# Separate row buffers for every other batch of q and k, in memory that the first batch's rows leave, and later places for the loads and DMA transposes

## The chip, the cores and the metric

One Trainium2 chip, one core of it. The metric is the device time of one launch in microseconds (us). The kernel before takes 309.26 us, the median of three runs (307.13 to 311.13).

## What is computed

Attention with a sliding window, and then a two-layer projection of all tokens. From the reference:

```python
# q, k, v: (8 batches, 8 heads, 576 positions, 64)
scores = scale * np.matmul(q, k.transpose(0, 1, 3, 2))
mask = np.abs(pos[:, None] - pos[None, :]) <= 32
attn = softmax(np.where(mask, scores, -1e9))
attn_out = np.matmul(attn, v)
...
x = attn_out.transpose(0, 2, 1, 3).reshape(4608, 512)
h = x @ w_in                                   # 512 -> 2048
g = where(h >= 1, h, where(h <= -1, 0, (h + 1) ** 2 / 4))
out = g @ w_out                                # 2048 -> 512
```

## The kernel before, in words

**One main loop.** The loop variable `a` at line 497 counts 144 steps of projection work (18 blocks of 256 tokens, 8 steps a block) and 16 more for the rest of the output. A step multiplies a piece of the hidden layer (lines 491 or 516), brings it through ScalarE and VectorE (lines 535 to 542), and then issues the attention work that is entered for this step and a few matmuls of the second layer (line 451 in `unit`). The attention of batch b is thus spread over the projection of the batches before it. The order of every engine's instructions is written out by hand: `at(a, ...)` enters work for a step, and `run(a)` issues it.

**Where q and k come from.** Scores need q and k with head dimension on the partitions: the tiles `qT` (three of them, in turn) and `kT` (three). For batch 0 and 1 TensorE transposes the rows. For batch 2 to 7 the way has two parts:

- `load_nat(b, t)` (line 95) loads the rows of q (t = 0) or k (t = 1) in their natural order into a tile `qn` or `kn` of 4,608 bytes a partition, with two DMAs (line 99) from the POOL queue; each also casts float32 to bfloat16. `load_v` (line 102) loads v with four DMAs.
- `xpose(b, t)` (line 196) turns such a tile into `qT` or `kT` with one DMA transpose (line 198) from the SP queue.

The scores of a batch (line 231) are the readers of `kT`. The first of them for batch 2 to 7 stand in steps 26, 38, 52, 68, 86 and 104.

**Where the work is entered.** For batch 3 to 7 the loads of q, k and v are entered at the step of that batch's first scores less 17, 16 and 15; the two transposes 6 and 8 steps after the first of these, which is 11 and 9 steps ahead of the first scores. The transposes of batch 2 stand at steps 16 and 18, and its loads ahead of the loop. POOL does nothing in the loop but issue loads, so the step of a load does not hold it back: POOL issues loads one after the other, each as soon as its buffer is free. The SP queue issues two things, in program order: the transposes, and the DMAs of finished output (`out`, lines 456 and 472). Each output DMA waits for the ScalarE copy (`osb`, lines 455 and 471) that makes its data. Output DMAs of the part that matters are entered in steps 27, 31, 35, 39, 45, 50, 55, 61, 66, 71, 75, 79 and every fourth after that. Inside a step the output comes ahead of the transpose.

**Row buffers.** There are two buffers for q and k rows, tags `n0` and `n1`. The tag is `n{(b + t) % 2}`, so q of batch b takes the buffer in which k of batch b-1 was, and k of batch b that of q of batch b-1. A load of batch b therefore waits for the transposes of batch b-1. `vn` has three buffers, so v of batch b waits for the last attention work of batch b-3.

**Batch 0's memory.** A pool named `early` holds what only the start needs: the rows of batch 0 (`q32`, `qh`, `kh`, `qb`) and a small tile `step`, together about 16.6 KB a partition. It stays open to the end of the kernel. Its last readers are the TensorE transposes of step 1.

Of the kernel before, what the change touches and what calls it, by code (L numbers as in the profile page):

```python
# [8 lines left out]
BF = mybir.dt.bfloat16  # L9
# [5 lines left out]
def kernel(  # L15
# [20 lines left out]
    B, H, S, D = q.shape  # L36
# [3 lines left out]
    NU = NY * S // 128  # L40
# [8 lines left out]
    nat = ctx.enter_context(tc.tile_pool(name="nat", bufs=2))  # L49
# [26 lines left out]


    qn, kn, vn = {}, {}, {}
    HD = (slice(0, 64), slice(64, 128))

    def load_half(half, t, h, eng=None, x=None):
# [12 lines left out]

    def load_nat(b, t):
        src, dst, nm = ((q, qn, "qn"), (k, kn, "kn"))[t]
        x = dst[b] = nat.tile([128, NU, 2, D], BF, name=nm, tag=f"n{(b + t) % 2}", bufs=1)
        for h in range(2):
            nc.gpsimd.dma_start(out=x[:, :, h], in_=src[b, NY * h:NY * h + NY].rearrange("y s d -> (y s) d")  # L99
                                .rearrange("(u p) d -> p u d", p=128))  # L100

    def load_v(b, n):
        if b not in vn:
            vn[b] = nat.tile([128, 2 * NC, 2, D], BF, name="vn", tag="vn", bufs=3)
        h, a = divmod(n, 2)
        y = NY * h + 2 * a
        nc.gpsimd.dma_start(out=vn[b][64 * a:64 * a + 64, :, h], in_=v[b, y:y + 2].rearrange("y s d -> (y s) d")  # L107
                            .rearrange("(c r) d -> r c d", r=64))
# [8 lines left out]
        nc.gpsimd.dma_start(out=w_out[:, k0:k1, 256 * c:256 * c + 256],  # L117
                            in_=moe_w_out.rearrange("(ko ki) f -> ki ko f", ki=128)[:, k0:k1, 256 * c:256 * c + 256])

    early = ctx.enter_context(tc.tile_pool(name="early", bufs=1))  # L120
    q32 = early.tile([128, 2, S], FP, name="q32")
    for h in range(2):
        load_half(0, 0, h, (nc.sync, nc.scalar)[h], q32)
# [21 lines left out]
    def put(todo):  # L145
        for fn, *x in todo:
            fn(*x)
# [7 lines left out]
    put([(load_v, 1, n) for n in range(4)])  # L155
    P.tensor_copy(band[HD[1], 0:128], band[HD[1], 64:192])
    for m, n, x in ((mask4, 8, 128), (mask8, 4, TAIL)):
        P.tensor_copy(m.rearrange("p (n j) -> p n j", n=n),
                      band[:, :x].rearrange("p (n j) -> p n j", n=1).to_broadcast([128, n, x]))
    put([(load_w_out, 1, 8 * n, 8 * n + 8) for n in range(2)])  # L160
    put([(load_nat, 2, t) for t in range(2)] + [(load_v, 2, n) for n in range(4)])


# [9 lines left out]
    def tpose(b, n, t, copy, ps):  # L173
# [14 lines left out]
        for j in range(j0, j1):  # L188
            if isinstance(src, list):
                for h in range(2):  # L190
                    nc.tensor.transpose(ps[HD[h], j - j0], src[h][:, D * j:D * j + D], ident)  # L191
            else:
# [3 lines left out]
    def xpose(b, t):  # L196

        nc.sync.dma_start_transpose(out=qkT(b, t).rearrange("d (u p) -> d u p", p=128),
                                    in_=(qn, kn)[t][b].rearrange("p u h d -> p (u h d)"))
# [7 lines left out]
    def add_mask(ps, n, w):  # L207
        for a in range(2):
            for h in range(2):
                nc.tensor.matmul(ps[h][HD[a], :n * w].rearrange("p (n j) -> p n j", n=n), ident[HD[h], HD[h]],  # L210
                                 bias[HD[h], 64 * h:64 * h + w].rearrange("p (n j) -> p n j", n=1)
                                 .to_broadcast([64, n, w]),
                                 start=True, stop=False, skip_group_check=True)

    def scores(b, ys, pars, cs, eng, pool=ps_s, w=128, ready=None):
# [8 lines left out]
        for y1 in range(*ys):  # L224
            for par in range(*pars):
                for c2 in range(*cs):
                    c = 2 * c2 + par
                    for a in range(2):
                        for h in range(2):
                            s0 = S * (y1 + 2 * a) + 64 * c  # L230
                            nc.tensor.matmul(ps[HD[a], h, w * n:w * n + w], kT[b][HD[h], s0:s0 + 64],  # L231
                                             qTs[b % 3][HD[h], PAD + s0 - 32:PAD + s0 - 32 + w],
                                             start=eng is not None, stop=True, skip_group_check=True)
# [81 lines left out]
    def flush():  # L315
        while muls:
            muls.pop(0)()
# [9 lines left out]
    def tposes(b, *sets):  # L327

        todo = []
        for (t, half), pool, copy in zip(sets, (ps_s, ps_n), (A.copy, V.tensor_copy)):  # L330
            tp = pool.tile([128, 2, 8, 128], BF, name="tp", tag="bb")
            todo += [tpose(b, 2 * half + part, t, copy, tp[:, part]) for part in range(2)]
        for copy in todo:
            copy()
# [78 lines left out]
    sl = [30, 32, 35, 38, 41, 44, 47, 50, 52, 57, 60, 63, 66, 68, 72, 76, 79, 82, 86]  # L413
# [4 lines left out]
        at(10 + 1.5 * t, (tposes, 1, (t, 0), (t, 1)))  # L418
    loads, xps = {}, {16: [(2, 0)], 18: [(2, 1)]}
    for b in range(LONG + 1, B):  # L420
        a = sl[5 * (b - 1) - 7] - 17
        for t in range(3):
            loads.setdefault(a + t, []).append((b, t))
        for t in range(2):
            xps.setdefault(a + 6 + 2 * t, []).append((b, t))
# [3 lines left out]
    def home(t):  # L429

        return (3 - t % 4 if t % 4 in (0, 3) else t % 4) if WIDE[0] <= NF * t < WIDE[1] else t % 4
# [43 lines left out]
    def run(pos):  # L475
        todo = []
        for fn, *x in ev.get(pos, []):
            if fn is sums:
                todo.append(sums(*x))
            elif fn is tposes:  # L480
                tposes(*x)
            else:
                pool = (x.pop(),) if x[-1] in (ps_s, ps_n, ps_o) else ()
                fn(*x, eng, *pool)
        for end in todo:
            end()

    def project(hp, f, r0, todo, first, last):

        for n, (j, kk) in enumerate(todo):  # L490
            nc.tensor.matmul(hp[:, j], w_in[:, kk, 256 * f + 128 * j:256 * f + 128 * j + 128],  # L491
                             xT[:, kk, r0:r0 + TB], start=first and n == 0, stop=last and n == len(todo) - 1,
                             skip_group_check=True)
# [3 lines left out]
    for a in range(NF * NB + 2 * NF):  # L497
        wide = WIDE[0] <= a < WIDE[1]
        eng = None if a < 14 else V
        post = [] if a >= 40 else [x for n, x in pairs if n == a] + [a - NF] * (a >= 2 * NF + 2)  # L500
        for b, x in loads.get(a, []):
            if x < 2:
                load_nat(b, x)
            else:
                for n in range(4):
                    load_v(b, n)
        if a == 0 or a > 3:
            flush()
        if a < NF * NB:
            if wide:  # L510
                n, f = divmod(a - WIDE[0], 2 * NF)
                t = WIDE[0] // NF + 2 * n
                r0 = TB * t % RING
                hp = ps_h.tile([128, 2, TB], FP, name="hp", tag="hp")
                for n, kk in enumerate((0, 2, 1, 3)):
                    nc.tensor.matmul(hp.rearrange("p n t -> p (n t)"), w_in[:, kk, 128 * f:128 * f + 128],  # L516
                                     xT[:, kk, r0:r0 + 2 * TB], start=n == 0, stop=n == 3)
                g = gT[:, f, home(t):home(t + 1) + 1:home(t + 1) - home(t)]
            else:
                t, f = divmod(a, NF)  # L520
                r0 = TB * t % RING
                if a in (0,):
                    hps = [ps_h.tile([128, 2, TB], FP, name="hp", tag="hp") for _ in range(2)]
                    for y in range(2):
                        for n in range(2):
                            project(hps[n], f + n, r0, [(j, y + 2 * m) for j in range(2) for m in range(2)], y == 0, y == 1)
                elif not hps:
                    pool, tag = (ps_o, "op") if a == 6 else (ps_h, "hp")
                    hps = [pool.tile([128, 2, TB], FP, name="hp", tag=tag)]
                    project(hps[0], f, r0, [(j, kk) for j in range(2) for kk in (0, 2, 1, 3)], True, True)  # L530
                hp = hps.pop(0)
                g = gT[:, 2 * f:2 * f + 2, home(t)]

            rr = ewp.tile([128, 2, TB], FP, name="rr")
            A.activation(rr, hp, AF.Relu, scale=0.5, bias=0.5)  # L535
            mx = ewp.tile([128, 2, TB], FP, name="mx")
            if a in two_on_act:
                A.activation(mx, rr, AF.Square)
                V.scalar_tensor_tensor(g, hp, 1.0, mx, op0=ALU.max, op1=ALU.min)
            else:  # L540
                V.tensor_max(mx, hp, rr)  # L541
                V.scalar_tensor_tensor(g, rr, 1.0, mx, op0=ALU.min, op1=ALU.mult)  # L542
        flush()
        run(a)
        for x in post:
            if x < 16:
                pair(x)
            else:
                for j in range(4):
                    unit(4 * x + j)  # L550
        if a >= 40:
            n = 3 if a < 72 else 4
            for x in range(done, done + n):
                unit(x)
            done += n
        run(a + 0.5)
        for x in xps.get(a, []):
            xpose(*x)

# [29 lines left out]
```

## Time and profile before

| | |
|---|---|
| runs | 307.13, 309.26, 311.13 us |
| the profiled execution: its own time | 308.08 us |
| its span, first to last instruction | 306.3 us |
| granted TensorE clock | 1.0 throughout |
| ACT, POOL busy | 190.6 us, 78.2 us |
| bytes moved by DMA | 35.67 MB |

The span is what the trace shows; 1.8 us of the execution's time lie outside it. "Busy" is time in which an engine ran an instruction; for POOL and SP the issuing of DMAs lies on the queue's sequencer. A row of the chain of waits or of the list of waits such as `PE bb L231 <- DMA kT<-kn` says that TensorE stood still ahead of line 231 until a DMA that writes `kT` from `kn` had landed. In a list of waits the numbers are the total in us, how often, and the longest.

### The profile page before, as it was taken

How to read it: one execution, taken by the hardware profiler on the slowest of the kernel's cores; microseconds unless marked ns; L12 is line 12 of the kernel's file. 1: busy time of each engine (PE TensorE's matmuls, PEld its weight loads, DVE VectorE, ACT ScalarE, POOL GpSimd, SP SyncE). 2: the span in 40 equal slices, each digit the busy share in tenths (PEclk: the TensorE clock that was granted, in tenths of full speed). 3: DMA queues.
4: the chain of work that ended last, by engine and by line, in shares of the span. 5: the costliest groups of instructions: out<-in, count | busy, mean ns of one | idle time of the engine just before them, and what ended most of it. 6: DMA issues, size and time to landing. Idle time of an engine off the chain costs nothing.

```text
span 306.3 us, 7848 instructions
## 1 busy us (share of the span) xinstructions
PE 298.4 (97%) x3324; PEld 175.0 (57%) x3324; DVE 241.8 (79%) x378; ACT 190.6 (62%) x318; POOL 78.2 (26%) x94
## 2 busy tenths in 40 slices
PE   8889999999999999999999999999999999999995
PEld 3567878876666776544444444444445444446644
DVE  4278958879888999999988888888888888788700
ACT  3687796648757767667766766665667654444311
POOL 8896661037008204601800730000000000000000
PEclk9999999999999999999999999999999999999999
DMA  9999999989999996997999997551011000000121
GB/s 153 184 195 201 178 185 179 165 152 159 127 155 145 151 142 122 171 155 121 147 154 177 108 170 77 113 112 36 34 36 37 34 36 35 34 36 34 58 81 68
DMA packets 137331, 35.67 MB, mean 116 GB/s; under 512 B 122320, under 2 KB 133072, under 8 KB 137296
## 3 DMA queue, kind: packets, MB, share of 16 engines
q0 software_dynamic: 103136, 18.06, 80.2%
q1 hardware_dynamic: 34016, 16.81, 26.8%
q8 instruction: 26, 0.43, 0.6%
q10 hardware_dynamic: 144, 0.29, 0.4%
q14 instruction: 9, 0.07, 0.1%
HBM read 36.70 MB, written 9.44 MB: 151 GB/s over the span
## 4 chain that ended last, share of the span: by engine, by line
PE 85%; DMA 8%; POOL 3%; ACT 1%; issue 1%; DVE 0%; POOLq 0%; ACTq 0%
PE op L451 34%; PE hp L516 23%; PE hp L491 14%; DMA kT<-kn 7%; PE bb L297 5%; PE op L466 5%; PE bb L231 2%; DMA w_in<-in_moe_w_in_dram 2%; POOL w_in L112 1%; PE op L442 1%; POOL vn L107 1%; PE tp L191 1%; POOL kh L86 1%; POOL qh L86 0%; PE bb L210 0%
## 5 line engine op out<-in xcount | busy, mean ns | idle before, releaser
L535 ACT ACTIVATE rr<-hp 128x512 f32<-128x512 f32 x144 | 85.5, 595 | 84.5 <-PE hp L516 49.5
L451 PE MATMUL op<-w_out,gT 128*128 128x512 bf16 x496 | 126.9, 380 | 0.0
L541 DVE TENSOR_TENSOR mx<-hp,rr 128x512 f32<-128x512 f32 x139 | 95.8, 689 | 26.7 <-ACT rr L535 24.9
L542 DVE SCALAR_TENSOR_TENSOR gT<-rr,mx 128x512 bf16<-128x512 f32 x139 | 96.4, 694 | 4.8
L516 PE MATMUL hp<-xT,w_in 128*128 128x512 bf16 x320 | 82.1, 379 | 0.0
L451 PEld LDWEIGHTS <-gT 128*128 128x128 bf16 x496 | 46.1, 98 | 47.6
L491 PE MATMUL hp<-xT,w_in 128*128 128x256 bf16 x512 | 66.2, 273 | 1.7 <-DMA w_in<-in_moe_w_in_dram 1.5
L491 PEld LDWEIGHTS <-w_in 128*128 128x128 bf16 x512 | 49.2, 98 | 17.0 <-DMA w_in<-in_moe_w_in_dram 1.3
L516 PEld LDWEIGHTS <-w_in 128*128 128x128 bf16 x320 | 31.3, 98 | 37.8
L99 POOL DMA_DIRECT2D qn<-in_q_dram x12 | 14.6, 1222 | 92.2 <-DMA kT<-kn 90.1
L239 ACT ACTIVATE pt<-bb 128x1024 bf16<-128x1024 f32 (+1 forms) x33 | 32.9, 1002 | 6.1 <-PE bb L231 4.7
L107 POOL DMA_DIRECT2D vn<-in_v_dram x32 | 27.5, 893 | 5.1 <-DMA w_out<-in_moe_w_out_dram 2.9
L309 DVE TENSOR_TENSOR xT<-bb,rc 128x512 bf16<-128x512 f32 (+1 forms) x32 | 21.0, 657 | 9.8 <-ACT rc L304 8.9
L455 ACT COPY osb<-op 128x512 f32<-128x512 f32 x31 | 18.0, 581 | 12.4 <-PE op L451 12.1
L304 ACT ACTIVATE rc<-lr 128x512 f32<-128x512 f32 (+2 forms) x40 | 23.5, 587 | 1.3
L303 ACT ACTIVATE lr<-bb 128x512 f32<-128x512 f32 (+2 forms) x40 | 22.0, 550 | 0.2
L205 DVE TENSOR_TENSOR pt<-pt,mask 128x1024 bf16<-128x1024 bf16 (+1 forms) x33 | 20.3, 615 | 0.8 <-ACT pt L239 0.7
L297 PE MATMUL bb<-pt,ones 64*64 64x256 bf16 (+3 forms) x352 | 19.5, 255 | 0.2 <-DVE xT L309 0.2
L297 PE MATMUL bb<-pt,vn 64*64 64x128 bf16 (+3 forms) x712 | 18.3, 204 | 0.0
L297 PEld LDWEIGHTS <-ones 64*64 64x64 bf16 x352 | 10.2, 106 | 12.9 <-issue 12.8
L297 PEld LDWEIGHTS <-vn 64*64 64x64 bf16 x712 | 16.7, 107 | 0.1
L466 PE MATMUL op<-w_out,gT 128*128 128x256 bf16 x128 | 16.3, 273 | 0.0
(61 smaller groups left out, 139.2 us busy)
## 6 DMA issues: line engine op xcount, KB each, us to landing
out_dram<-osb SPq DMA_DIRECT2D x35, 256.0 KB, 2.7
vn<-in_v_dram POOLq DMA_DIRECT2D x32, 144.0 KB, 11.4
qn<-in_q_dram POOLq DMA_DIRECT2D x12, 288.0 KB, 7.0
kn<-in_k_dram POOLq DMA_DIRECT2D x12, 288.0 KB, 9.4
w_in<-in_moe_w_in_dram POOLq DMA_DIRECT2D x11, 128.0 KB, 5.0
w_out<-in_moe_w_out_dram POOLq DMA_DIRECT2D x4, 256.0 KB, 8.0
w_out<-in_moe_w_out_dram POOLq DMA_DIRECT2D x2, 512.0 KB, 12.4
kh<-in_k_dram POOLq DMA_DIRECT2D x4, 144.0 KB, 4.7
```

The costliest lines, as they stand in the source:

```text
L107: nc.gpsimd.dma_start(out=vn[b][64 * a:64 * a + 64, :, h], in_=v[b, y:y + 2].rearrange("y s d -> (y s) d") .rearrange("(c r) d -> r c d", ...
L239: A.activation(p, ps[:, :, :w * n].rearrange(like, y=m), AF.Exp, scale=D ** -0.5)
L297: nc.tensor.matmul(bb[HD[h], a, o + c0:o + c1], ones[HD[a]] if c is None else vn[b][HD[a], c, h], p(a, h), start=n == 0, stop=True, skip_g ...
L303: A.activation(lr[:, :, :D0], bb[:, :, D0:2 * D0], AF.Ln)
L304: A.activation(rc[:, :, :D0], lr[:, :, :D0], AF.Exp, scale=-1.0)
L451: nc.tensor.matmul(op[tt], gT[:, j, home(tt // 2), 128 * (tt % 2):128 * (tt % 2) + 128], w_out[:, j], start=j == 0, stop=j == 15)
L466: nc.tensor.matmul(o[:, tt], gT[:, j, p, 128 * tt:128 * tt + 128], w_out[:, j, 256 * half:256 * half + 256], start=not done, stop=len(done ...
L491: nc.tensor.matmul(hp[:, j], w_in[:, kk, 256 * f + 128 * j:256 * f + 128 * j + 128], xT[:, kk, r0:r0 + TB], start=first and n == 0, stop=l ...
L516: nc.tensor.matmul(hp.rearrange("p n t -> p (n t)"), w_in[:, kk, 128 * f:128 * f + 128], xT[:, kk, r0:r0 + 2 * TB], start=n == 0, stop=n == 3)
L535: A.activation(rr, hp, AF.Relu, scale=0.5, bias=0.5)
L541: V.tensor_max(mx, hp, rr)
L542: V.scalar_tensor_tensor(g, rr, 1.0, mx, op0=ALU.min, op1=ALU.mult)
```

## The change

Even batches keep their rows in the pool `nat`, with one buffer for q (tag `n0`) and one for k (`n1`). Odd batches get two buffers of the same size in a new pool `nat2`. The pool `early` is closed at the end of step 1, and `nat2` is opened there, in the memory that `early` leaves (9.2 KB a partition of the 16.6). A load of batch b then follows the transpose of the same tensor of batch b-2, and for batch 3 the last readers of batch 0's rows. The loads and the transposes of batches 3 to 7 are entered two steps later than before: transposes at 29 and 31 instead of 27 and 29 for batch 3, 43 and 45 for batch 4, 59 and 61 for batch 5, 77 and 79 for batch 6, 95 and 97 for batch 7. The loads and transposes of batch 2 are where they were. `int()` around the list entry changes nothing, since the entries used are whole numbers.

```diff
     qn, kn, vn = {}, {}, {}
+    nats = [nat]
...
     def load_nat(b, t):
         src, dst, nm = ((q, qn, "qn"), (k, kn, "kn"))[t]
-        x = dst[b] = nat.tile([128, NU, 2, D], BF, name=nm, tag=f"n{(b + t) % 2}", bufs=1)
+        x = dst[b] = nats[b % 2].tile([128, NU, 2, D], BF, name=nm, tag=f"n{t}", bufs=1)
...
-    early = ctx.enter_context(tc.tile_pool(name="early", bufs=1))
+    stack = ExitStack()
+    early = stack.enter_context(tc.tile_pool(name="early", bufs=1))
...
     for b in range(LONG + 1, B):
-        a = sl[5 * (b - 1) - 7] - 17
+        a = int(sl[5 * (b - 1) - 7]) - 15
         for t in range(3):
             loads.setdefault(a + t, []).append((b, t))
...
         run(a + 0.5)
+        if a == 1:
+            stack.close()
+            nats.append(ctx.enter_context(tc.tile_pool(name="nat2", bufs=1)))
         for x in xps.get(a, []):
             xpose(*x)
```

## The prediction

> **What bounds the kernel now.** I read the busy line and the slices of the page first, then the list of waits, then the timelines of SP and PE around the waits found.
>
> ```profile
> PE 298.4 (97%) x3324; PEld 175.0 (57%) x3324; DVE 241.8 (79%) x378; ACT 190.6 (62%) x318; POOL 78.2 (26%) x94
> PE   8889999999999999999999999999999999999995
> DMA  9999999989999996997999997551011000000121
> ```
>
> PE is busy 97% of the span, and each slice from the fourth to the last but one is full. The DMA engines are full for the first half. So DMA is the second limit, and it can cost time only where PE waits for it.
>
> ```profile
> POOL qn L99 <- DMA kT<-kn: 90.1, 5, 19.3
> PEld L231 <- DMA kT<-kn: 1.1, 2, 0.6
> PE bb L231 <- DMA kT<-kn: 0.8, 2, 0.4
> ```
>
> The large number is POOL's: five times it holds the next batch's loads until the last transpose of the batch before has landed. POOL has nothing else to do then. What PE loses by late `kT` is two stalls. PEld and PE record the same two, so they are not added. The timeline of PE has both:
>
> ```profile
> 92.33 0.42 PE L231 MATMUL bb<-qT,kT 64*64 64x128 bf16 x16 [0.41 <-DMA kT<-kn]
> 118.74 0.42 PE L231 MATMUL bb<-qT,kT 64*64 64x128 bf16 x16 [0.44 <-DMA kT<-kn]
> ```
>
> These are the first scores of batches 3 and 4: 0.41 + 0.44 = 0.85 us. **That is all this wait costs PE.** The chain of waits gives `kT<-kn` 7% only because it books the whole flight of two transposes (9.55 and 10.91 us), during which PE worked. From the same timeline I take when PE reaches each batch's first scores with nothing in the way, the deadlines of `kT`: batch 2 at 67.65, 3 at 92.33 - 0.41 = 91.92, 4 at 118.30, 5 at 147.02, 6 at 181.29, 7 at 216.42 us. SP's timeline for batch 3:
>
> ```profile
> 71.05 0.34 SPq L456 DMA_DIRECT2D out_dram<-osb  x1
> 74.92 7.65 SPq L198 DMA_TRANSPOSE qT<-qn  x1
> 82.74 5.99 SPq L198 DMA_TRANSPOSE kT<-kn  x1
> 88.83 1.00 SPq L456 DMA_DIRECT2D out_dram<-osb  x2
> ```
>
> SP is free at 71.4 but issues `qT` only at 74.92, when `qn` has landed (74.76); issuing one transpose then holds SP for 6 to 7.7 us. ScalarE's copy for the output of step 31 is done at 78.52 + 0.59 = 79.1, yet that output leaves at 88.8, behind `kT`.
>
> **What the Trainium skill says.** The page "DMA: Bandwidth & Descriptors", section "Queues, rings and completion order", says that each DMA engine goes round-robin between the queues that have work for it. The trace agrees. The DMA view of 100 to 104 us, loads alone, and of 134 to 136 us, loads beside transposes (packets, MB, share):
>
> ```profile
> q0 software_dynamic: 4689, 0.60, 256.4%
> ```
>
> ```profile
> q1 hardware_dynamic: 829, 0.21, 79.9%
> q0 software_dynamic: 830, 0.10, 79.7%
> ```
>
> Loads alone make 4,689/4 = 1,172 packets a us; beside transposes each side makes 415. The section "Two DMAs through the same engine are not ordered" says that descriptors of one queue start in order; the landings agree, since batch 3's q, k and v, issued from 66.5 on in this order, land from 72.8 to 88.8 in this order. The section "Anatomy of one DMA" says that a semaphore is waited for on the issuing sequencer before dispatch; the output held to 88.8 agrees. Finally "Trainium Kernel Development and Optimization", section "Best Practices", advises double buffers to lay DMA beside compute; here PE is already covered but for 0.85 us, so the advice has that much left to win.
>
> **Part one, the buffers.** Loads of batch b no longer wait for `kT` of b-1. POOL, free at 47.2 after batch 2's last v, can go on with batch 3 instead of waiting until 66.54. The waits there show POOL stopping for landings that no buffer needs (`w_out` ahead of a v load), which I read as about eight loads in flight at most; batch 2's first landed at 48.3, so batch 3 starts there. It goes behind batch 2's loads in the queue, whose last landed at 63.99, so it flows from 64 on. A batch has 4 x 2,304 + 4 x 1,152 = 13,824 packets (the 64-element rows of the q, k and v loads), 11.8 us alone. Batch 3's q lands near 70 (3.5 us at 415 a us, then the other 3,150 packets at 1,172) instead of 74.8; batch 4's start near 67 to 70, when batch 2's transposes free their buffers. POOL waits elsewhere; nothing but loads stands behind it. The price: transposes will seldom have the engines to themselves. Closing and opening pools issues no work; its waits fall on POOL, long after step 1 (19 us). I take 0, with a bound of 0.1 us.
>
> **Part two, two steps later.** SP doesn't know steps; only an output that now comes ahead of a transpose delays it. Batch 3: `qT` still follows the output of step 27 and, with q landed, goes at 71.4, 3.5 us earlier. `kT` now follows step 31's output, ready at 79.1, or `qT`'s issue, 71.4 + 7.65 = 79.05: it goes at 79.9 at the latest, against 82.74. Batch 4: `qT` follows step 39's output, at 96.5 instead of 101.2. `kT` follows that of step 45, whose copy starts at 106.44 and takes 0.58: 107.2 against 107.79. Batch 5: `qT` near 125.5 instead of 127.4; `kT` behind step 61's output (copy at 135.41) at 136.1 instead of 133.60. Batch 6: `kT` behind step 79's at 171.2 instead of 165.0. Batch 7: both behind step 95's, near 201 and 204.
>
> **From issue to landing.** Under load `kT` took 8.8, 9.6, 10.9 and 9.9 us (batches 2 to 5), always just behind `qT`; `qT`, first in its pair, took 13.7, 13.9, 13.5 and 12.7. Without load either takes 4.6 to 5.6 (batches 6, 7). In the changed kernel `kT` of 3 and 4 follows `qT` at a distance, with more loads beside it. I choose midway between the means 9.8 and 13.5, 11.7 us, with both as bounds.
>
> - Batch 3: 79.9 + 11.7 = 91.6, deadline 91.92: no stall, gain 0.41. Bounds: gain 0.41, or 93.4 and a stall of 1.5.
> - Batch 4: 107.2 + 11.7 = 118.9, deadline 118.30: stall 0.6 where 0.44 was. Bounds: none, or 120.7 and 2.4.
> - Batch 5: 136.1 + 8.3 (midway between 4.9 and 11.7, as only part of batch 7's load is beside it) = 144.4, deadline 147.02: none. Bounds: none, or 147.8 and 0.8.
> - Batches 6 and 7: 171.2 + 5 and 204 + 5.6 stay 5 and 7 us ahead. No cost unless 10 us are needed: cover for both.
> - Batch 2: its transposes were alone after 63.99. With batch 3's loads behind, the roughly 1,270 transpose packets that the trace has after 64 us take 1,270/415 = 3.1 us instead of some 1.4: landing 65.83 becomes 67.5, deadline 67.65: none. Bounds: none, or 1.0.
>
> Sum: -0.85 + 0.6 = -0.2 us (rounded). PE has the same matmuls and no other change; outputs leave earlier, for which nobody waits. **308.08 - 0.2 = 307.9 for the profiled execution**, which lies 1.2 us under the median shown: 309.1 in the terms of that median.
>
> **The rivals.** *Every `kT` in time*: both stalls go and none comes: -0.85 us, 308.4. For it: the loads land well ahead. Against: more loads beside each transpose. It is the ceiling, because PE waits nowhere else for these rows.
>
> *The loads are not earlier*, if POOL is still held by something: then only SP's order changes, each of batch 3's and 4's `kT` waits some 0.4 us for the issue of one output, +0.8: 310.1. Against: the memory of batch 0 has been read by 19 us.
>
> *Slower: transposes starve in a queue of loads that never drains.* If `kT` takes the 13.9 us that `qT` of batch 3 took, the stalls are 79.9 + 13.9 - 91.92 = 1.9, then 2.8, 3.0, and 1.0 in batch 2: 8.7 - 0.85 = +7.9, 317. For it: `qT` did take so long, and landed each time only when the v loads had landed (88.82 and 88.80, 114.69 and 114.53). Against: packets alternate one to one, and batch 5 has slack. It decides by 2% from about 13.4 us a `kT` (three flights less the 34.0 us from issue to deadline, plus 0.15, reach 6.2).
>
> **How the numbers follow.** This kernel's runs differ by 1.3%, so 2% is what can be told from no change. I give the forecast (a sum within some 3 us of nothing) 0.62, every `kT` in time 0.17, no earlier loads 0.08, starving 0.13, of which 0.10 beyond 2%. The first three lie within 2%. For faster by 2%, 6 us would have to go where PE waits 0.85: 0.03, for what I have not seen. The range takes the in-time case less the runs' own 2 us, 306.4, up to the forecast's bounds: stalls of 1.5 + 2.4 + 0.8 + 1.0 give +4.9 when all are bad, 314; I stop at 313.2, and most of starving lies outside.
>
> **What would show it.** Right: POOL's first load of batch 3 near 48; `qT` of batch 3 near 71.4 with no wait of SP for `qn`; `kT` near 80, 107 and 136; PE's stalls before line 231 of one us or so in all; PE busy 298 us still. Wrong: `kT` flights above 13 us, stalls of several us in batch 3 to 5, or POOL still idle until 66. A stall of PE on anything but `kT` would mean that I missed a reader.

## The result: slower, and the profile after

The changed kernel takes 320.98 us, the median of six runs (319.05 to 324.25), against 309.24 us of the kernel before on the same chip: a ratio of 1.0379, with a 95% interval of 1.0315 to 1.0444. The ratio leaves out the longest run, 324.25 us, which was in a slow state, over 1.5% above the shortest. The profiled execution took 319.96 us, its span 318.2 us, 11.85 us more than the span before (318.16 against 306.32). The forecast was 309.1 us and 313.2 at most.

The busy line and the slices of the page of the changed kernel:

```profile
PE 295.5 (93%) x3286; PEld 176.0 (55%) x3324; DVE 242.1 (76%) x378; ACT 190.7 (60%) x318; POOL 78.2 (25%) x94
...
PE   8789999959996997799999999999999999999995
...
PEclk9999999998999999799999999999999999999999
DMA  9999999999999999999999580028010000000021
```

PE has holes in three places where it was full, at the ninth, the thirteenth and the sixteenth and seventeenth slice, and beside two of them the granted clock dips as well. The DMA engines are now full for longer on end. 38 of PE's matmul records are missing from this trace (3,286 against 3,324), so its busy time is not to be compared to the microsecond. The list of waits, TensorE's and POOL's rows on these rows and tiles:

```profile
POOL qn L100 <- DMA qT<-qn: 27.5, 3, 10.6
...
POOL kn L100 <- DMA kT<-kn: 26.1, 3, 11.7
...
PE bb L233 <- DMA kT<-kn: 9.7, 3, 3.8
```

POOL waits less for transposes, 54 us where it was 90. PE waits more: three times, 9.7 us in all, where it was twice and 0.8 us. The timeline of PE has the three stalls (start, length, engine, line and operation; in brackets the idle time ahead of it and what ended it):

```profile
71.02 0.64 PE L233 MATMUL bb<-qT,kT 64*64 64x128 bf16 x16 [3.21 <-DMA kT<-kn]
...
99.45 0.42 PE L233 MATMUL bb<-qT,kT 64*64 64x128 bf16 x16 [2.72 <-DMA kT<-kn]
...
129.24 0.64 PE L233 MATMUL bb<-qT,kT 64*64 64x128 bf16 x16 [3.82 <-DMA kT<-kn]
```

They are the first scores of batches 2, 3 and 4. After the first and the third the same 16 matmuls take 0.64 us, not 0.42. The windows of PE around the three stalls (length, busy time and instructions, granted clock, DMA share, GB/s) say why:

```profile
67.27:70.68 3.41, 0.53 (x29) 1.00 1.82 163
70.68:74.09 3.41, 2.85 (x25) 0.50 1.79 224
94.58:97.99 3.41, 2.16 (x41) 1.00 1.77 118
97.99:101.40 3.41, 1.79 (x26) 1.00 2.21 195
101.40:104.81 3.41, 3.41 (x26) 1.00 2.68 152
125.30:128.71 3.41, 0.12 (x16) 1.00 2.84 152
128.71:132.12 3.41, 2.55 (x23) 0.50 1.20 128
```

Twice the clock is granted at half for a stretch of 3.41 us. The first stretch begins 0.34 us before its stall ends, the second 0.53 us before. PE works through the other 3.07 and 2.88 us (the view has less, since records are missing), and half of each is lost. **This accounts for the difference between the two profiled executions:** stalls of 3.21 + 2.72 + 3.82 = 9.75, less the 0.85 us that were there before, plus (3.07 + 2.88)/2 = 2.98 for the clock: 11.88 us against the 11.85 measured. From batch 5 on the two kernels run in step. The other five runs of the changed kernel have mean clocks of 0.977 to 0.989, where the profiled one has 0.989. One stretch of 3.41 us at half takes 0.005 off the mean, so I estimate two to four such stretches in a run.

Why `kT` is late is to be seen on SP's timeline:

```profile
75.36 0.34 SPq L458 DMA_DIRECT2D out_dram<-osb  x1
76.02 7.46 SPq L200 DMA_TRANSPOSE qT<-qn  x1
83.94 0.34 SPq L458 DMA_DIRECT2D out_dram<-osb  x1
84.45 7.66 SPq L200 DMA_TRANSPOSE kT<-kn  x1
```

`kT` of batch 3, issued at 84.45, landed at 99.41: 15.0 us in flight, where it flew 9.55 before. `kT` of batch 2, issued at 57.1 in both kernels, flew 13.85 us instead of 8.8; that of batch 4 14.5 instead of 10.9.

### The profile page after: what moved, and what is told of

Read it like the earlier page. It is cut to its first block, busy times and chain, and to the rows that moved or that the text cites. A ratio compares the mean times of both kernels' runs of the same rounds, so it can differ in the third digit from the quotient of the medians.

```text
span 318.2 us, 7813 instructions
## 1 busy us (share of the span) xinstructions
PE 295.5 (93%) x3286; PEld 176.0 (55%) x3324; DVE 242.1 (76%) x378; ACT 190.7 (60%) x318; POOL 78.2 (25%) x94
## 4 chain that ended last, share of the span: by engine, by line
PE 66%; DMA 25%; POOL 3%; issue 2%; SPq 2%; ACT 0%; POOLq 0%; ACTq 0%
PE op L453 30%; PE hp L518 22%; DMA kT<-kn 14%; PE hp L493 7%; DMA qn<-in_q_dram 4%; DMA w_out<-in_moe_w_out_dram 4%; PE bb L299 4%; SPq L200 2%; DMA w_in<-in_moe_w_in_dram 2%; PE bb L233 2%; DMA vn<-in_v_dram 2%; POOL w_in L113 2%; PE op L444 1%; POOL kh L87 1%; POOL qh L87 0%
## 5 line engine op out<-in xcount | busy, mean ns | idle before, releaser
L453 PE MATMUL op<-w_out,gT 128*128 128x512 bf16 x460 | 120.2, 381 | 5.4 <-issue 5.2
L544 DVE SCALAR_TENSOR_TENSOR gT<-rr,mx 128x512 bf16<-128x512 f32 x139 | 96.4, 693 | 4.8
L493 PE MATMUL hp<-xT,w_in 128*128 128x256 bf16 x512 | 67.5, 276 | 1.8 <-DMA w_in<-in_moe_w_in_dram 1.1
L311 DVE TENSOR_TENSOR xT<-bb,rc 128x512 bf16<-128x512 f32 (+1 forms) x32 | 21.0, 657 | 10.2 <-ACT rc L306 9.3
L233 PE MATMUL bb<-qT,kT 64*64 64x128 bf16 (+1 forms) x520 | 13.4, 222 | 10.0 <-DMA kT<-kn 9.7
L100 POOL DMA_DIRECT2D kn<-in_k_dram x12 | 14.5, 1212 | 31.1 <-DMA kT<-kn 26.1
L299 PEld LDWEIGHTS <-ones 64*64 64x64 bf16 x352 | 10.2, 106 | 12.5 <-issue 12.5
```

What stands on the lines that cost most here:

```text
L299: nc.tensor.matmul(bb[HD[h], a, o + c0:o + c1], ones[HD[a]] if c is None else vn[b][HD[a], c, h], p(a, h), start=n == 0, stop=True, skip_g ...
L453: nc.tensor.matmul(op[tt], gT[:, j, home(tt // 2), 128 * (tt % 2):128 * (tt % 2) + 128], w_out[:, j], start=j == 0, stop=j == 15)
```

## Experiments

Two things changed, which rows are loaded when, and where the transposes stand on SP's queue. The first three kernels take them apart. All ratios are to the kernel before, run on the same chip (308.14 us beside the first three and the last, 307.76 us beside the others). "Theory A" is that loads in flight beside the transposes slow them down; "B" that their place on SP's queue does.

**The buffers alone.** The changed kernel with the old steps:

```diff
-        a = int(sl[5 * (b - 1) - 7]) - 15
+        a = int(sl[5 * (b - 1) - 7]) - 17
```

> The changed kernel with the loads and transposes at their old steps (qT and kT of batches 3 to 5 go one right after the other, no output between). Theory A, contention: the earlier loads fill the DMA engines while the transposes fly. Then batch 2 is as in the changed kernel, kT landing near 71 us and a stall of PE of about 3.2 us with the clock at half after it; kT of batch 3 lands near 96 to 98; whole time 312 to 317 us. Theory B, order: the two steps put kT behind outputs and this is what makes it late. Then 308 to 310 us, and batch 2, which the steps do not touch, would have no stall.

Measured: 313.58 us, ratio 1.0184 (1.0130 to 1.0239). The timeline of PE, and its windows around the end of the stall:

```profile
70.84 0.42 PE L233 MATMUL bb<-qT,kT 64*64 64x128 bf16 x16 [2.84 <-DMA kT<-kn]
```

```profile
68.57:71.98 3.41, 1.14 (x24) 1.00 1.70 210
71.98:75.39 3.41, 3.41 (x15) 0.50 2.29 176
```

Batch 2 stalls by 2.84 us and the clock is halved for 3.41 us, from 71.98 on, with none of the changed steps in this kernel: A for this stall. Batches 3 and 4 do not stall, though `kT` flies 13.5 and 13.9 us. PE was 4.7 and 4.1 us behind by then and reached these scores at 96.63 and 122.41; `kT` landed at 96.04 and 122.36, just ahead of it.

**The steps alone.** The kernel before with `- 15` for `- 17`.

> The kernel before with the loads and transposes of batches 3 to 7 two steps later, and the old two buffers. Theory A, contention: loads still wait for the transposes of the batch before, kT flies 9 to 11 us as before, and only the issue of an output comes ahead of it: 308.5 to 311 us, stalls of 1.0 to 2.0 us in all. Theory B, order: 316 to 322 us, with stalls in batches 3 and 4 of 2 to 4 us each.

Measured: 309.46 us, ratio 1.0046 (1.0027 to 1.0064). `kT` of batches 3 and 4 flies 9.5 and 10.3 us; PE waits for them 1.4 us in two stalls, 0.6 us more than before:

```profile
PE bb L231 <- DMA kT<-kn: 1.4, 2, 0.7
```

B explains half a per cent, not 3.8.

The two parts alone make 1.8 and 0.5%, together 3.8. I put the rest down to what the first experiment shows to be at the edge: with loads beside it, `kT` of batches 3 and 4 has 0.6 us and less than 0.1 us to spare, and the later place takes more than that. In the changed kernel batch 4's `kT` is issued at 114.67, behind an output, not at 108.45 straight behind `qT`.

**Buffers and steps, loads at their old times.** The changed kernel with one copied element on POOL, which has to wait for `kT` of the batch before:

```diff
         x = dst[b] = nats[b % 2].tile([128, NU, 2, D], BF, name=nm, tag=f"n{t}", bufs=1)
+        if t == 0 and b > 2:
+            P.tensor_copy(x[0:1, 0, 0, 0:1], kT[b - 1][0:1, 0:1])
```

> The changed kernel, buffers in the new memory and the later steps, with one copy of one element on POOL ahead of each batch's loads, from kT of the batch before into the new tile, so that the loads start when they did before. Theory A, contention: batch 2 has no stall, kT flies 9 to 11 us, 308.5 to 311 us. Rival C, that the memory or the closing of the pool costs the time, and rival B, order: 316 to 322 us.

Measured: 309.68 us, ratio 1.0053 (1.0032 to 1.0074). POOL's timeline:

```profile
67.36 0.18 POOL L100 COPY qn<-kT 1x1 bf16<-1x1 bf16 x1 [19.20 <-DMA kT<-kn]
```

POOL stands still for 19.2 us again, batch 2 has no stall, and the flights are 8.7, 9.7 and 9.7 us. Two stalls are left, in batches 3 and 4:

```profile
PE bb L235 <- DMA kT<-kn: 2.3, 2, 1.3
```

The memory of batch 0, the closed pool and the new buffers cost nothing that shows; the time is that of the later steps alone, within the intervals. It is the time at which the loads run that costs.

**Only batch 3's loads early.** As above, with `b > 3` for `b > 2`.

> The changed kernel with the held loads of the earlier experiment for batches 4 to 7 alone, so that only batch 3's loads come early. Theory A, contention: batch 2 stalls as in the changed kernel, 3.2 us and 1.5 us by the half clock; in batch 3 the loads have drained by 83 us and kT issued near 84.5 lands by 93, with no stall; batch 4 at most 1 us. Whole time 311.5 to 314.5 us. Rival: the late kT of batches 3 and 4 comes from PE's shift in batch 2 and from kT's place behind an output, without the loads: 316 to 321 us.

Measured: 311.55 us, ratio 1.0128 (1.0076 to 1.0181). SP's timeline:

```profile
85.83 0.34 SPq L460 DMA_DIRECT2D out_dram<-osb  x1
86.34 2.80 SPq L202 DMA_TRANSPOSE kT<-kn  x1
```

Here too `kT` of batch 3 follows an output, and PE is behind by batch 2's stall (2.99 us, then half clock for 6.8 us). But batch 3's loads have landed by 83.5 us, and `kT` issued at 86.34 lands at 91.02, after 4.7 us. No stall in batch 3 or 4. So those two stalls need the loads of the next batch; batch 2's shift and the place on SP's queue alone do not make them. The four runs of this kernel also price the half clock: with mean clocks of 0.999 and 1.000 they took 310.72 and 310.99 us, with 0.995 312.12 us, and with 0.989 (the profiled one) 313.55 us. By these four runs a stretch of 3.41 us at half costs some 1.3 us.

**Fewer loads.** The changed kernel without the v loads of batches 3 to 7, which use batch 2's v instead:

```diff
-                for n in range(4):
-                    load_v(b, n)
+                vn[b] = vn[2]
```

> The changed kernel with the v loads of batches 3 to 7 left out (these batches use batch 2's v), a third fewer load packets. Theory A, contention: batch 2 stalls as before by 3 us, since q and k of batch 3 are in the queue alike; kT of batches 3 and 4 flies 7 to 12 us instead of 15, with 0 to 1 us of stall each: 311 to 315 us. If the number of loads in flight did not matter: flights of 14 to 15 us and 319 to 322 us.

Measured: 313.1 us, ratio 1.0171 (1.0121 to 1.0220). `kT` of batches 3 and 4 flies 12.1 and 10.2 us and PE does not stall for them; batch 2 stalls by 2.75 us. Between all loads (15.0, 14.5) and the last kernel below (5.2, 5.7) this is a middle dose, and the flights are in the middle.

**PE kept busy.** The changed kernel with matmuls on zeros in the stalls:

```diff
+        if b in (2, 3, 4) and ys[0] == cs[0] == 0:
+            keep_warm(12, ps_h, "hp")
         ps = ready or two_banks(pool)
```

> The changed kernel with 12 matmuls of 128x512 on zeros (0.216 us each at full clock, 2.6 us) ahead of the first scores of batches 2, 3 and 4, where PE stood still for 3.2, 2.7 and 3.8 us; they add no data to anything. If PE's idle stretch of about 3 us is what sets its clock to half for the 3.4 us after it: the granted clock is 1.0 throughout, the first matmuls after the scores take 0.22 us again, and 2 to 3 us go, 317 to 319 us. Rival: the half clock comes from something else in these places, such as the DMA load. Then the clock is still halved twice and the time is 320 to 323 us.

Measured: 320.15 us, ratio 1.0384 (1.0334 to 1.0434), so the gain did not come. The windows around batch 2's and batch 4's first scores:

```profile
68.00:72.00 4.00, 3.33 (x41) 1.00 1.76 169
72.00:75.00 3.00, 2.85 (x35) 1.00 1.79 221
126.00:130.50 4.50, 1.74 (x9) 1.00 2.83 130
130.90:134.30 3.40, 3.40 (x17) 0.50 1.12 79
```

In batch 2 the matmuls left 0.77 us of idle time, and the clock stayed at 1.0 after it: with the 12 matmuls the half clock after this stall is gone. In batch 4 `kT` flew 16.2 us this time, so that 2.78 us of idle time were left behind the matmuls, and the clock was halved. So the trace bears out that idle time is what halves the clock: where the matmuls filled it the clock stayed, where they did not it fell. The times show no gain. In the profiled execution, at 321.53 us the longest of the four, what was won in batch 2 was lost to the longer flight and to a start that was 0.9 us later. But the mean clocks of the four runs are 0.992 to 1.000, above all runs of the changed kernel, and their times are no shorter; why stays open.

**Transposes with the engines to themselves.** The kernel before, with v held until `kT` of the same batch has landed:

```diff
             vn[b] = nat.tile([128, 2 * NC, 2, D], BF, name="vn", tag="vn", bufs=3)
+            if b > 1:
+                P.tensor_copy(vn[b][0:1, 0, 0, 0:1], kT[b][0:1, 0:1])
...
-    put([(load_nat, 2, t) for t in range(2)] + [(load_v, 2, n) for n in range(4)])
+    put([(load_nat, 2, t) for t in range(2)])
...
-    loads, xps = {}, {16: [(2, 0)], 18: [(2, 1)]}
+    loads, xps = {19: [(2, 2)]}, {16: [(2, 0)], 18: [(2, 1)]}
...
-            loads.setdefault(a + t, []).append((b, t))
+            loads.setdefault(a + (t if t < 2 else 9), []).append((b, t))
```

> The kernel before with v of batches 2 to 7 loaded after kT of the same batch has landed (one copied element on POOL holds it), so that no load is in flight beside most transposes. Theory A, contention: kT lands 5 to 6 us after its issue, 4 us or more ahead of its deadline in every batch, no stall of PE at line 231, 307.5 to 309 us, that is 0 to 0.5 per cent under before. If the loads beside the transposes are not what makes them slow: flights of 9 to 11 us stay, and 309 to 311 us.

Measured: 307.88 us against 308.14, ratio 0.9999 (0.9983 to 1.0015). SP's timeline of batch 3:

```profile
75.60 4.27 SPq L200 DMA_TRANSPOSE qT<-qn  x1
80.04 3.39 SPq L200 DMA_TRANSPOSE kT<-kn  x1
```

`kT` flies 4.6 to 5.7 us in every batch (5.2 here: it lands at 85.25, more than 6 us ahead of its deadline). Beside the transposes of 79 to 83 us there is next to no load (packets, MB, share):

```profile
q1 hardware_dynamic: 2266, 0.57, 117.5%
...
q0 software_dynamic: 29, 0.00, 1.4%
```

PE has no stall for these `kT` any more. That is A at its cleanest, and as a version it is no better than the kernel before: the 0.85 us that it takes away do not show in the times, whose interval reaches to -0.17%, a little short of the -0.28% that they would be. In the profiled execution the start, up to 40 us, was 1.1 us later than in that of before; such shifts, 0 to 1.5 us, are in the profiles here. Whether this alone hides the gain was not tried.

## Why the prediction was wrong, by its own steps

**What held.** PE is the bound and POOL's 90 us cost nothing: POOL now waits 36 us less for transposes and the kernel is slower. POOL issued batch 3's first load at 49.2 (near 48 was said). SP no longer waits for `qn` (0.8 us in all, 10.5 before). The order on SP came out: behind PE's shift of 4.8, 7.1 and 11.8 us, `kT` at 79.9, 107.2 and 136.1 would be at 84.7, 114.3 and 147.9, and is at 84.45, 114.67 and 148.29. The price of the later places without early loads, set at 0.8 us, is 1.4 us as measured by itself (0.46% of 308, with an interval from 0.8 to 2.0 us). The bound of 0.1 us for the pools stands unshaken: the gated kernel is no slower than the later steps alone, within the intervals, which are wider than that bound. Two small things did not hold: the output that left at 88.8 was held by the issue of `kT` ahead of it and by the wait of `qT` for `qn`, not by a semaphore of its own, and the chances, with the 0.03 for faster, add up to 1.03.

**The step that failed: "From issue to landing".** It gave `kT` of batches 3 and 4 11.7 us, with 13.5 as the bound, and they took 15.0 and 14.5. The ends of the bound were read as "under load", and the lower one was not. Some 1,830 of the 2,304 packets of batch 3's `kT` moved after 88.0 us, when hardly a load was left. The DMA view of the kernel before at 88 to 92 us, the second half of batch 3's `kT`:

```profile
q1 hardware_dynamic: 1948, 0.65, 110.3%
...
q0 software_dynamic: 12, 0.00, 0.5%
```

and of the changed kernel at 94 to 96 us, in the midst of the same transpose:

```profile
q1 hardware_dynamic: 802, 0.21, 85.9%
q0 software_dynamic: 802, 0.10, 77.3%
```

The v load of batch 3 landed at 88.80 and `kT` had the engines for itself; with batch 4's rows behind it, each queue gets its turn to the end. In the packets of the changed kernel `kT` of batch 3 takes 5.8 us from issue to the first packet, 7.3 us for its 2,304 and 1.8 us to landing; in the kernel before it was 4.0, 4.75 and 0.8 us. In both the wait for the first packet is for the most part `qT` still moving (all of the 4.0 us, 4.4 of the 5.8). My own rate of 415 a us says 5.6 us for the packets; the rest is in part a stretch from 96.4 to 97.1 us in which both queues nearly stood still, and no run here tells why. A flight with loads beside it to the last packet was there to be read: `qT` of batch 3 before, 4.5 + 7.3 + 2.1 = 13.9 us. Such a sum, not a midpoint of old flights, would have been the estimate to make; it still lies 1.1 and 0.6 us under what was measured.

**Batch 2** failed by the same step in a smaller form. "The roughly 1,270 transpose packets after 64 us" were what was left after a stretch in which the loads had already run thin. The view of the kernel before at 62 to 64 us, and of the changed kernel at 66 to 68:

```profile
q1 hardware_dynamic: 929, 0.23, 85.6%
q0 software_dynamic: 316, 0.04, 31.0%
```

```profile
q1 hardware_dynamic: 826, 0.21, 79.9%
q0 software_dynamic: 827, 0.11, 79.8%
```

Batch 3's loads fill this stretch too: `kT` lands at 70.97, not 67.5, and its bound of 1.0 us of stall became 3.2. It came without any changed step and brought the half clock with it, 4.7 us in all, so it made every later deadline and issue late.

**What was missing altogether** is that a stall can cost more than its length: 2.98 of the 11.85 us are TensorE at half clock. No stall before was long enough to show it.

**The rivals.** The slower one, "transposes starve in a queue of loads that never drains", named the place and nearly the price, 13.9 us a flight with a decision at 13.4. Its 0.13 was too little. Its word was wrong: nothing starves, packets go one to one (802 and 802); a flight with its share from the first packet to the last is enough. Its stalls of 1.0, 1.9, 2.8 and 3.0 us in batches 2 to 5 were 3.2, 2.7, 3.8 and none, so that its 8.7 us in all came near the 9.75 partly by luck, and the clock was not in it. The argument against it, "batch 5 has slack", held, by 0.1 us: `kT` of batch 5 landed at 158.78, and PE, 11.8 us late, came to it at 158.86.

The Trainium skill's sentence on round-robin queues ("DMA: Bandwidth & Descriptors", "Queues, rings and completion order") was the right ground, and for the transposes was applied to one batch only. The advice to double buffers ("Trainium Kernel Development and Optimization", "Best Practices") is not at fault either: what it buys, a load ahead of time, PE had no use for, and the engines that carry the load carry the transposes too.

## What to carry to other kernels

A buffer that makes a queue wait can be what keeps two kinds of DMA apart; before it is freed, ask what will then be in flight together, and which of the two has the nearer deadline. A flight time measured before holds only for the neighbours that it had: split it into the wait for its first packet, its packets at the shared rate and the landing, and price each for the new neighbours. Where PE has less than a microsecond of stalls, no more than that is to be won by moving transfers, and here 12 us were to be lost.

## What was not expected of the hardware

- The granted clock changed only at marks 3.41 us apart: in all nine traces the stretches on record are whole multiples of it (19, 1, 16, 1 and 55 in the changed kernel) up to the last, which the end of the program cuts short. The clock was 0.5 after windows between two marks in which PE was idle for 2.19 us (only batch 3's loads early), 2.27 (buffers alone), 2.75 (fewer loads), 2.78 (kept busy) and 2.88 and 3.29 us (changed kernel, batches 2 and 4). Batch 3's stall in the changed kernel, 2.72 us long, lay across the mark at 97.99: PE was idle for 1.25 us before and 1.62 us after it, as the windows in the section on the result show, and the clock stayed at 1.0. The length of a stall alone does not fit: with only batch 3's loads early, the clock fell when the stall was 2.19 us old. So the same stall can cost half clock or not by where it lies between the marks. Where between 1.62 and 2.19 us of idle time the limit lies is not shown. With only batch 3's loads early the half clock lasted for two windows, 6.83 us, with 0.95 us of idle time in the first.
- Loads alone made 1,172 packets a us; loads and transposes side by side 830 together, 415 each. The pair moves fewer packets than the loads alone, but about as many bytes (0.31 MB in 2 us against 0.60 in 4), since a transpose's packet here has 256 bytes and a load's 128.
- With loads in flight a `qT` had its first packet 4.5 to 5.5 us after issue in batches 2 to 4 (both kernels), with none 1.25 us. No run here tells what holds it.
- In none of the nine traces was a load issued from POOL with more than seven earlier ones in flight. In the changed kernel there were seven at nearly every issue from 20 to 107 us, so the loads hardly ever drained.
